# Seeding a PSUM accumulation with a ScalarE copy in place of a VectorE addition

## The chip, the core and the metric

The kernel runs on one core of a Trainium2 chip. TensorE (PE in the rows) multiplies matrices and writes PSUM; its weight loads are listed apart as PEld. VectorE (DVE) and ScalarE (ACT) work on SBUF and PSUM, GpSimd (POOL) on SBUF, and SyncE (SP) issues most transfers. Each engine takes its own instructions in order and waits on semaphores for the others. The metric is the device time of one execution in microseconds, the median of three runs.

## What is computed

The input `x` has the shape 4 x 3072 x 256. A two-dimensional Fourier transform over the last two axes gives 3072 tokens of 256 values in each of 4 batches. Two blocks of products follow:

```
X = fft(fft(x, axis=1), axis=2).real
xk = mu_k * X + (1 - mu_k) * X_prev        # X_prev: the token before
xr = mu_r * X + (1 - mu_r) * X_prev
k = max(xk @ w_k, 0)                       # 256 -> 1024
y = sigmoid(xr @ w_r) * (k * k @ w_v)      # 1024 -> 256
h = y @ w_in                               # 256 -> 2048
out = (h - tanh(h)) @ w_out                # 2048 -> 256
```

## The kernel before, in words

The Fourier transform comes first (to some 90 us). Phase 1 (some 95 to 640 us) computes `y`, phase 2 (to the end) computes `out`. Both phases go through 12 pairs of token blocks; a pair is two blocks of 512 tokens. A **step** is one call of `quad`: it makes a 2 x 2 set of result blocks, called 11, 12, 21 and 22, of the first product (`w_k` or `w_in`) with seven block products in the manner of Strassen and Winograd. Phase 1 has 4 steps for each pair, 48 in all; phase 2 has 8, 96 in all. Each block product is taken in split precision: `P(...)` issues three matmuls of 128 x 512 (lines 395 to 397), high times high, high times low, and low times high.

Every result block is bent (`bend`, L571: ReLU in phase 1, tanh in phase 2, by ScalarE), gated by VectorE (L635 for block 11, L664 for 22, L686 for 21, L687 for 12), and split into a high half by ScalarE (`hi`, L576) and a low half by VectorE (`lo`, L578). Then `second` multiplies it with the second weight (`w_v` or `w_out`): 6 matmuls for each block, into the banks `o`. `second` runs one step behind: what a step issues is its own first products, and, between these, the second products of the step before (`p`).

The order on each engine is the order in which the code is written; nothing reorders it. `self.fill()` puts the preparation of later work (splits of the left operands, weight conversion, mixing) at fixed points of the step.

The names that matter for this change:

- `X` is a PSUM bank (two of them take turns, `x0` and `x1`). It first takes the product `a11`, later `s2`, `s3` and `a22` are accumulated onto it.
- `Z` is a PSUM bank, and there is one of it only (`bank("z", "z")`). A step uses it twice: for block 11 and, from L660 on, for block 22. The last reader of block 22 is its low half, L578 `m<-z,m`; until that has run, the next step may not write `Z`.
- `s1` is an SBUF tile. L593 copies the product `a11` from `X` to it (ScalarE), before `s2` is added onto `X`.
- Block 11 is `a11` + `a12`: the product `a12` goes into `Z`, and L610 (VectorE) adds `s1` to it.

On TensorE a step begins with `a11` into `X` (3 matmuls), then the 6 matmuls of `second(p, "11")`, then `a12` into `Z` (3), then `s2` onto `X` (3). On ScalarE the copy L593 stands behind the bend of the last step's block 21 (L571 `c<-x`), and that, in phase 1, behind the high half of block 22 and what `fill` put there.

Of the kernel before, what the change touches and what calls it, by code (L numbers as in the profile page):

```python
# [392 lines left out]
def mm3(T, ps, w, m, start=True, stop=True):  # L393

    T.matmul(ps, w[0], m[0], start=start, stop=False, skip_group_check=True)  # L395
    T.matmul(ps, w[0], m[1], start=False, stop=False, skip_group_check=True)  # L396
    T.matmul(ps, w[1], m[0], start=False, stop=stop, skip_group_check=True)  # L397
# [9 lines left out]
class Kernel:  # L407
# [148 lines left out]
    def quad(self, ph, n, q, nq, S, W, w2, done, extra=None):  # L556
# [3 lines left out]
        V, A, T = self.V, self.A, self.T  # L560
        ALU, ACT = mybir.AluOpType, mybir.ActivationFunctionType
        M = {}
        def P(ps, k, start, stop=True):
            i = RIGHT[k]
            mm3(T, ps, [W[:, 0, i], W[:, 1, i]], [S[k][:, 0], S[k][:, 1]], start, stop)
        bank = lambda tag, name: self.ps.tile([128, TOK], F32, tag=tag, name=name, bufs=1)
        ctile = lambda: self.act.tile([128, TOK], F32, tag="c", name="c", bufs=4)
        stile = lambda: self.act.tile([128, TOK], F32, tag="s", name="s", bufs=3)
# [11 lines left out]
        def late(*names):  # L580
            for k in names:
                if p:
                    p["late"][k]()
        self.odd ^= 1
        X, Z = bank(f"x{self.odd}", "x"), bank("z", "z")
# [3 lines left out]
            late("t21", "g21")  # L589
        else:  # L590
            late("t21", "c12", "g21")
        s1 = stile()
        A.copy(s1, X)  # L593
        if p is None:
            self.fill()
        if ph == 1:
# [1 line left out]
        else:  # L598
            late("t12", "h21", "g12")
        self.second(p, "11")  # L600
        P(Z, "a12", True)
        Wb = None
        late("l21")
        if ph == 2:
# [2 lines left out]
        if p is None:  # L607
            Wb = bank("w", "w")
            P(Wb, "s1", True)
        V.tensor_add(Z, Z, s1)  # L610
        if ph == 2:
            late("l12")
        s2 = stile()
# [41 lines left out]
        if p is None:  # L655
            P(X, "a22", False)
            P(Wb, "s4", False)
            Z = Y
# [420 lines left out]
```

## Time and profile before

| | |
|---|---|
| median of three runs | 1638.91 us (1638.88 to 1639.13) |
| span of the profiled execution | 1637.3 us |
| TensorE busy | 1624.5 us, 99% |
| VectorE busy | 1269.1 us, 78% |
| ScalarE busy | 1137.7 us, 69% |
| GpSimd busy | 583.8 us, 36% |
| phase 1, 120 to 636 us: TensorE, VectorE, ScalarE | 516.0, 437.3, 387.3 us |
| phase 2, 670 to 1618 us: TensorE, VectorE, ScalarE | 948.0, 689.6, 626.6 us |

The profiled execution spans 1637.3 us, 1.6 us less than the median, which also holds what lies around the span. Matmuls overlap: one lasts 0.39 us and the next starts 0.227 us after it, so the distance of the starts tells what one costs. An entry such as `[0.17 <-DVE m L578]` means that the engine stood still for 0.17 us before this instruction, until that one of VectorE had ended.

### The profile page before, as it was taken

The page shows a single profiled execution, that of the slowest core. Times are in us where ns is not written, and L with a number is a line of the kernel's source. Part 1 is how long each engine was busy: PE and PEld are TensorE (multiplying, and loading weights), DVE is VectorE, ACT ScalarE, POOL GpSimd, SP SyncE. Part 2 cuts the span into 40 slices and gives each one's busy share as a digit, 9 for nine tenths or more (in the row PEclk, how much of TensorE's full clock was granted, in tenths as well). Part 3 has the DMA queues.
Part 4 walks back from the last instruction along what each step waited for, and adds up shares of the span by engine and source line. Part 5 has one row for each costly group of instructions (what it writes and reads, how often), then busy time and mean ns, then how long its engine had stood idle before and what let it go on. Part 6 is the DMA issues. An engine that isn't in the chain of part 4 may idle for free.

```text
span 1637.3 us, 21326 instructions
## 1 busy us (share of the span) xinstructions
PE 1624.5 (99%) x7478; PEld 1349.2 (82%) x7478; DVE 1269.1 (78%) x1957; ACT 1137.7 (69%) x2171; POOL 583.8 (36%) x493
## 2 busy tenths in 40 slices
PE   8999999999999999999999999999999999999998
PEld 7978888888888887888888888888888888888887
DVE  7987888888898887777777777777777777777776
ACT  5887777777777777776666666666666666666665
POOL 1156676666676776462121212121202020202000
PEclk9999999999999999999999999999999999999999
DMA  9620111111111112301010101010101010101000
GB/s 334 173 65 27 46 46 52 33 46 58 46 66 53 58 56 67 103 14 52 1 52 1 52 1 52 1 52 1 52 1 52 1 52 1 52 0 52 1 26 26
DMA packets 39612, 78.76 MB, mean 48 GB/s; under 512 B 4672, under 2 KB 11328, under 8 KB 39504
## 3 DMA queue, kind: packets, MB, share of 16 engines
q1 hardware_dynamic: 37920, 72.94, 13.3%
q0 software_dynamic: 1440, 4.46, 1.6%
q8 instruction: 58, 0.95, 0.2%
q14 instruction: 50, 0.41, 0.1%
q10 hardware_dynamic: 144, 0.00, 0.0%
HBM read 45.86 MB, written 31.52 MB: 47 GB/s over the span
## 4 chain that ended last, share of the span: by engine, by line
PE 94%; DMA 2%; DVE 1%; ACT 1%; POOL 1%; issue 1%; SPq 0%; DVEq 0%; ACTq 0%; POOLq 0%
PE o L396 16%; PE o L397 16%; PE o L395 16%; PE x L395 8%; PE x L397 8%; PE x L396 8%; PE w L397 4%; PE w L395 4%; PE w L396 4%; PE z L395 2%; PE z L397 2%; PE z L396 2%; PE r L396 1%; PE r L397 1%; PE r L395 1%; PE s L217 1%
## 5 line engine op out<-in xcount | busy, mean ns | idle before, releaser
L578 DVE TENSOR_TENSOR m<-z,m 128x512 fp32r<-128x512 f32 x288 | 198.4, 689 | 141.1 <-ACT m L576 141.1
L696 POOL TENSOR_TENSOR a<-xk,a 128x512 fp32r<-128x512 f32 x70 | 93.0, 1332 | 591.1 <-ACT a L694 591.1
L396 PE MATMUL o<-m,WO 128*128 128x512 f32 x768 | 298.9, 389 | 0.0
L397 PE MATMUL o<-m,WO 128*128 128x512 f32 x768 | 298.8, 389 | 0.0
L395 PE MATMUL o<-m,WO 128*128 128x512 f32 x768 | 298.8, 389 | 0.0
L571 ACT ACTIVATE c<-z 128x512 f32<-128x512 f32 x288 | 173.0, 601 | 141.2 <-DVE z L660 140.8
L576 ACT CAST m<-z 128x512 fp32r<-128x512 f32 x288 | 169.3, 588 | 142.9 <-DVE z L664 80.2
L696 POOL TENSOR_TENSOR s<-xk,s 128x512 fp32r<-128x512 f32 x94 | 125.4, 1334 | 186.0 <-ACT s L694 182.7
L396 PEld LDWEIGHTS o<-m,WO 128*128 128x128 f32 x768 | 144.1, 188 | 30.3 <-DVE m L578 0.3
L395 PEld LDWEIGHTS o<-m,WO 128*128 128x128 f32 x768 | 144.1, 188 | 30.0
L397 PEld LDWEIGHTS o<-m,WO 128*128 128x128 f32 x768 | 144.1, 188 | 29.8
L396 PE MATMUL o<-m,wv 128*128 128x512 f32 x384 | 149.6, 389 | 0.1
L397 PE MATMUL o<-m,wv 128*128 128x512 f32 x384 | 149.5, 389 | 0.0
L395 PE MATMUL o<-m,wv 128*128 128x512 f32 x384 | 149.5, 389 | 0.0
L664 DVE TENSOR_TENSOR z<-z,c 128x512 f32<-128x512 f32 x144 | 100.3, 697 | 61.4 <-ACT c L571 60.3
L660 DVE TENSOR_TENSOR z<-w,s 128x512 f32<-128x512 f32 x143 | 99.9, 699 | 32.7 <-PE w L397 20.0
L593 ACT COPY s<-x 128x512 f32<-128x512 f32 x144 | 84.8, 589 | 56.4 <-PE x L397 56.2
L614 ACT COPY s<-x 128x512 f32<-128x512 f32 x144 | 84.6, 587 | 53.4 <-PE x L397 52.9
L635 DVE TENSOR_TENSOR z<-z,c 128x512 f32<-128x512 f32 x144 | 100.1, 695 | 24.1 <-ACT c L571 23.3
L686 DVE TENSOR_TENSOR x<-x,c 128x512 f32<-128x512 f32 x144 | 99.5, 691 | 10.6 <-ACT c L571 10.4
L687 DVE TENSOR_TENSOR c<-c 128x512 f32<-128x512 f32 x96 | 66.9, 696 | 49.8 <-ACT c L571 49.8
L578 DVE TENSOR_TENSOR m<-x,m 128x512 fp32r<-128x512 f32 x144 | 98.7, 686 | 2.7
(214 smaller groups left out, 4040.6 us busy)
## 6 DMA issues: line engine op xcount, KB each, us to landing
spill<-r SPq DMA_DIRECT2D x48, 256.0 KB, 2.5
xk<-spill SPq DMA_DIRECT2D x48, 256.0 KB, 5.4
out<-o SPq DMA_DIRECT2D x22, 512.0 KB, 2.6
raw<-w_in SPq DMA_DIRECT2D x32, 128.0 KB, 2.3
cv<-w_out SPq DMA_DIRECT2D x16, 256.0 KB, 3.5
wf<-wf SPq DMA_DIRECT2D x16, 256.0 KB, 2.7
xr<-x SPq DMA_DIRECT2D x3, 1024.0 KB
xr<-x SPq DMA_DIRECT2D x5, 512.0 KB
```

The costliest lines, as they stand in the source:

```text
L395: T.matmul(ps, w[0], m[0], start=start, stop=False, skip_group_check=True)
L396: T.matmul(ps, w[0], m[1], start=False, stop=False, skip_group_check=True)
L397: T.matmul(ps, w[1], m[0], start=False, stop=stop, skip_group_check=True)
L571: A.activation(t, src, ACT.Tanh if ph == 2 else ACT.Relu)
L576: A.copy(M[blk][:, 0], g)
L578: V.tensor_sub(M[blk][:, 1], g, M[blk][:, 0].bitcast(F32))
L593: A.copy(s1, X)
L635: gate(Z, Z, t11)
L660: V.tensor_add(Z, Wb, s3)
L664: gate(Z, Z, t22)
L686: g21=lambda: gate(X, X, st["t21"]), h21=lambda: hi("21", X), l21=lambda: lo("21", X),
L696: eng.tensor_sub(S[name][:, 1], src(), S[name][:, 0].bitcast(F32))
```

## The change

From the second step on, ScalarE copies the product `a11` from `X` straight into the bank `Z` (no tile `s1`), the three matmuls of `a12` are issued without the start flag, so that they accumulate on the copy, and the addition L610 is gone. The first step (`p is None`) stays as it was.

```
-        s1 = stile()
-        A.copy(s1, X)
+        if p is None:
+            s1 = stile()
+            A.copy(s1, X)
+        else:
+            A.copy(Z, X)
...
         self.second(p, "11")
-        P(Z, "a12", True)
+        P(Z, "a12", p is None)
...
-        V.tensor_add(Z, Z, s1)
+        if p is None:
+            V.tensor_add(Z, Z, s1)
```

Lines behind the change stand 3 or 4 further down: the copy is L596 in the changed kernel, L614 becomes L618, L635 becomes L639.

On TensorE, at the place where a step of phase 1 (the eleventh) multiplies `a12` into `z`. Before:

```order
L397 MATMUL o_2169<-m_2216,wv 128x512
L395 MATMUL z<-a_1804,TK 128x512 [waits DVE_49]
L396 MATMUL z<-a_1804,TK 128x512
L397 MATMUL z<-a_1804,TK 128x512
L395 MATMUL x<-s_1999,TK 128x512 [waits Activation_49]
```

The same place in the changed kernel:

```order
L397 MATMUL o_2152<-m_2198,wv 128x512
L395 MATMUL z<-a_1794,TK 128x512 [waits Activation_49]
L396 MATMUL z<-a_1794,TK 128x512
L397 MATMUL z<-a_1794,TK 128x512
L395 MATMUL x<-s_1985,TK 128x512
```

The order of the matmuls is the same; the wait for ScalarE has moved from the product `s2` three matmuls up to `a12`, and takes the place of a wait for VectorE.

On ScalarE, at the copy of the same step. Before:

```order
L576 CAST m_2260<-z 128x512 [waits DVE_49]
L694 CAST a_2264<-xk 128x512
L571 ACTIVATE c<-x 128x512 [waits PE_49,Activation_49]
L593 COPY s<-x 128x512 [waits PE_49,Activation_49]
L576 CAST m_2285<-x 128x512 [waits DVE_49]
L614 COPY s<-x 128x512 [waits PE_49,Activation_49]
```

The same place in the changed kernel:

```order
L576 CAST m_2242<-z 128x512 [waits DVE_49]
L698 CAST a_2246<-xk 128x512
L571 ACTIVATE c<-x 128x512 [waits PE_49,Activation_49]
L596 COPY z<-x 128x512 [waits DVE_49,PE_49]
L576 CAST m_2266<-x 128x512 [waits DVE_49]
L618 COPY s<-x 128x512 [waits PE_49]
```

The copy stands where it stood; it now also waits for VectorE, that is for the last reader of `z`.

## Rows read from the trace of the kernel before

**Rows 1.** The page: busy time, share and instructions of each engine.

```profile
PE 1624.5 (99%) x7478; PEld 1349.2 (82%) x7478; DVE 1269.1 (78%) x1957; ACT 1137.7 (69%) x2171; POOL 583.8 (36%) x493
```

**Rows 2.** Stretches of phases 1 and 2: length, busy time of each engine, PE clock.

```profile
120.00:636.00 516.00, 516.00 (x2272) 424.93 (x2271) 437.27 (x654) 387.34 (x720) 349.48 (x283) 1.00 0.15 50
670.00:1618.00 948.00, 948.00 (x4184) 784.97 (x4183) 689.58 (x1046) 626.60 (x1136) 182.26 (x151) 1.00 0.08 27
```

**Rows 3.** Waits of the weight loads: total us, times, longest.

```profile
PEld z L395 <- DVE m L578: 3.6, 15, 0.6
PEld x L395 <- ACT s L593: 2.0, 5, 0.7
```

**Rows 4.** Groups of ScalarE by line, phase 1, then phase 2: busy, mean ns | idle before.

```profile
L593 ACT COPY s<-x 128x512 f32<-128x512 f32 x47 | 27.8, 591 | 0.0
...
L593 ACT COPY s<-x 128x512 f32<-128x512 f32 x95 | 55.9, 588 | 56.2 <-PE x L397 56.2
```

**Rows 5.** Timeline of a step of phase 2: start, duration, engine, line, operation.

```profile
902.73 0.69 DVE L578 TENSOR_TENSOR m<-z,m 128x512 fp32r<-128x512 f32 x1
903.72 0.39 PE L397 MATMUL x<-a,TI 128*128 128x512 f32 x1
904.14 0.59 ACT L593 COPY s<-x 128x512 f32<-128x512 f32 x1 [0.45 <-PE x L397]
905.08 0.19 PEld L395 LDWEIGHTS z<-a,TI 128*128 128x128 f32 x1
```

**Rows 6.** Timeline of the eleventh step of phase 1.

```profile
207.10 0.59 ACT L593 COPY s<-x 128x512 f32<-128x512 f32 x1
207.19 0.68 DVE L578 TENSOR_TENSOR m<-z,m 128x512 fp32r<-128x512 f32 x1
207.93 0.19 PEld L395 LDWEIGHTS z<-a,TK 128*128 128x128 f32 x1 [0.17 <-DVE m L578]
208.27 0.39 PE L396 MATMUL z<-a,TK 128*128 128x512 f32 x1
208.51 0.59 ACT L576 CAST m<-x 128x512 fp32r<-128x512 f32 x1 [0.82 <-DVE x L686]
```

**Rows 7.** Timeline of phase 1, the tenth step, and one near the end.

```profile
196.29 0.59 ACT L593 COPY s<-x 128x512 f32<-128x512 f32 x1
196.44 0.39 PE L395 MATMUL z<-a,TK 128*128 128x512 f32 x1
...
590.36 0.59 ACT L593 COPY s<-x 128x512 f32<-128x512 f32 x1
590.51 0.39 PE L395 MATMUL z<-a,TK 128*128 128x512 f32 x1
```

**Rows 8.** Timeline of two more steps of phase 1.

```profile
172.24 0.69 DVE L578 TENSOR_TENSOR m<-z,m 128x512 fp32r<-128x512 f32 x1 [0.58 <-ACT m L576]
172.58 0.60 ACT L593 COPY s<-x 128x512 f32<-128x512 f32 x1
173.32 0.39 PE L395 MATMUL z<-a,TK 128*128 128x512 f32 x1
...
230.58 0.59 ACT L593 COPY s<-x 128x512 f32<-128x512 f32 x1
231.24 0.39 PE L395 MATMUL z<-a,TK 128*128 128x512 f32 x1
```

**Rows 9.** Timeline of the first step of phase 2.

```profile
649.17 0.19 PEld L395 LDWEIGHTS z<-a,TI 128*128 128x128 f32 x1 [0.44 <-DVE m L578]
649.71 0.58 ACT L593 COPY s<-x 128x512 f32<-128x512 f32 x1
650.35 0.19 PEld L395 LDWEIGHTS x<-s,TI 128*128 128x128 f32 x1 [0.65 <-ACT s L593]
650.68 0.39 PE L396 MATMUL x<-s,TI 128*128 128x512 f32 x1
```

**Rows 10.** Groups of VectorE by line, phase 1, then L681 in phase 2.

```profile
L610 DVE TENSOR_TENSOR z<-z,s 128x512 f32<-128x512 f32 x48 | 33.1, 689 | 0.0
L681 DVE TENSOR_TENSOR w<-w,s 128x512 f32<-128x512 f32 x47 | 32.3, 688 | 0.0
L687 DVE TENSOR_TENSOR w<-w,c 128x512 f32<-128x512 f32 x46 | 32.0, 696 | 19.4 <-ACT c L571 19.4
L660 DVE TENSOR_TENSOR z<-w,s 128x512 f32<-128x512 f32 x46 | 32.0, 696 | 18.7 <-PE w L397 18.7
...
L681 DVE TENSOR_TENSOR c<-w,s 128x512 f32<-128x512 f32 x96 | 66.2, 690 | 3.5
```

## Prediction

> **What bounds the kernel now.** I read the page first, then the busy time by stretch, then the waits of TensorE, then the timeline around the copy in both phases. TensorE is busy for 99% of the span [rows 1], and inside both phases without a break: 516.0 of 516.0 us and 948.0 of 948.0 us, at a granted clock of 1.00 (the 2.4 GHz level) [rows 2]. VectorE, at 78%, has room. So VectorE work that goes away gives nothing back by itself; only a wait of TensorE that goes or comes changes the time. Of such waits there are few around this place: the weight load of `a12` waits for the low half of block 22 in 15 steps, 3.6 us in all, and that of `s2` waits for the copy L593 in 5 steps, 2.0 us [rows 3]. Weight loads run ahead of the matmuls, so the matmuls lost less than that.
>
> The second thing to see is that the copy is a different thing in the two phases. In phase 2 ScalarE stands idle for 56.2 us in front of its 95 copies, waiting for the product: the copy starts as soon as it can. In phase 1 it is never idle in front of the 47 copies: they come late, out of a full queue [rows 4].
>
> **What goes.** 143 additions L610 of 0.689 us [rows 10] leave VectorE, 98.5 us in all. No TensorE wait names L610. Behind it in phase 1 VectorE waits 19.4 us in front of L687 for ScalarE, and 18.7 us in front of L660 for TensorE [rows 10]; the freed time turns into more of that idleness. I cost the removal at nothing; the cover is TensorE's unbroken row, and it needs no other. The bend of block 11, which read `Z` behind L610, stands in ScalarE's queue behind the next copies and starts when these are done.
>
> **What comes: a wait of TensorE for the copy.** Before, the copy had to be over by the product `s2`, three matmuls (0.68 us) behind `a12`. Now it has to be over by `a12` itself, and it may not begin until the low half of block 22 has read `Z`. Queued behind the waiting matmul is all of TensorE's work; behind the waiting copy, on ScalarE, the high half of block 21.
>
> The price of the hand-over comes from two places. In the eleventh step the low half ends at 207.19 + 0.68 = 207.87, and the second matmul of `a12` starts at 208.27 [rows 6]; one spacing of 0.227 earlier puts the first at 208.04, 0.17 after the release. In the first step of phase 2 the copy ends at 649.71 + 0.58 = 650.29 and the second matmul of `s2` starts at 650.68 [rows 9]: 650.45, again 0.16. I take 0.17.
>
> The copy itself now writes PSUM; no row of before shows ScalarE do that. The nearest rows are VectorE's addition L681, 688 ns into PSUM in phase 1 and 690 ns into SBUF in phase 2 [rows 10]: the destination makes no difference. I take the copy's own 0.59 us, with 0.50 and 0.63 as bounds (the addition's 0.69 is VectorE's own pace, so only part of that distance).
>
> The Trainium skill (Perfetto Trace Analysis, section Optimizing Scalar/DVE Operations) gives ScalarE an access overhead of about 93 ns on SBUF and 51 ns on PSUM, and says that the profiled latency holds about twice that; as an estimate from that page, the copy would take 0.51 to 0.55 us and the sum below would come out 2 to 4 us smaller. No row here shows ScalarE write PSUM, and the VectorE pair shows no such difference.
>
> *Phase 2, 95 steps behind its first.* The low half ends at 903.42, before the product is there; the copy starts at 904.14 and ends at 904.73; the weight load of `a12` comes at 905.08 [rows 5]. 0.35 us are left over, the hand-over to the weight load costs 0.06 (650.29 to 650.35 [rows 9]), so 0.29 is spare. The steps repeat every 10.20 us with the same numbers. Cost nothing, unless the copy grew beyond 0.88 us. Only the step after the first, at 659.6, has its copy late, by 0.29.
>
> *The first step of phase 2* already waits for the copy, at `s2` [rows 9]. The wait moves three matmuls up, so it costs these three: 0.68.
>
> *Phase 1, 47 steps.* I went through all 47 in the timeline; they are of four sorts.
> - 12 steps where the low half ends after the copy has begun and `a12` already waited for it, or nearly so [rows 6]. The copy moves behind the low half: 207.87 + 0.03 + 0.59 + 0.17 = 208.66, against 208.04 before: 0.62 late. On ScalarE the copy ends at 208.49, and the next instruction did not start before 208.51 anyway.
> - 15 steps where the copy begins just before `a12`: 196.29 + 0.59 + 0.17 = 197.05 against 196.44, 0.61 late; likewise 590.36 + 0.76 = 591.12 against 590.51 [rows 7].
> - 11 steps with part of that: 172.93 + 0.03 + 0.59 + 0.17 = 173.72 against 173.32, 0.40 late [rows 8].
> - 9 steps with next to nothing: 230.58 + 0.76 = 231.34 against 231.24, 0.1 late [rows 8]; four of the nine not late at all.
>
> Where `s2` already waited for the copy only the shift of 0.68 counts. With that the first two sorts, 27 steps, give 16.8 us (0.62 each), the 11 give 4.2 (0.38 each), the 9 give 0.5: 21.5 us for phase 1.
>
> Does a step's lateness stay lost, or does ScalarE catch up while TensorE stands? The copy of the next step hangs on a chain that starts behind the place of the stall: L660 waits for TensorE's `w` (18.7 us of idle time in 46 steps [rows 10]), then come bend, gate, high half, the filled-in cast, the bend of block 21, and the copy. When TensorE is 0.6 us late this chain starts 0.6 us late too. So each step pays anew, and I take the sum as it is.
>
> **The sum.** 21.5 + 0.7 + 0.3 = 22.5 us. The stalls that were counted among [rows 3] and now lie under the copy's wait are mostly taken off above; I round down to 22. Against the profiled execution: 1637.3 + 22 = 1659.3 us of span; with the 1.6 us around it, 1661 us beside the median of 1638.9: 1.3% slower. A copy of 0.50 us takes 0.09 off some 43 late steps, 3.9 us; one of 0.63 adds 1.7. A chain that runs faster by 0.15 us a step, because VectorE's queue in front of L660 is shorter, takes off up to 7; more collisions with filled-in work may add 3. That makes 11 to 27 us, 1650 to 1666.
>
> **The rivals.**
> - *VectorE's relief pulls the chain forward, not slower.* In about half the steps of phase 1 L660 shows no idle time, so VectorE's queue may be what it starts from. If the removed 0.69 us came off there, low half, bend and copy would all come up to 0.69 us earlier, just as much as they are now late. It decides from 0.6 us a step on; then all but the ends vanish: 0 to 3 us, 1639 to 1642. Against it: the 19.4 us that VectorE waits in front of L687 [rows 10] lie between the removed addition and L660, so the time is lost before it gets there. 5%.
> - *Only half of it: partial relief together with a short copy.* If the chain came 0.25 us earlier in all steps and the copy took 0.50, the 27 steps keep 0.28 each (7.6) and the rest nearly nothing: 8 to 9 us with the ends, 1647. 8%.
> - *The copy into PSUM is so slow that phase 2 waits too.* It takes a copy beyond 0.88 us. At 1.0 us phase 1 pays 0.41 more in 43 steps (18 us) and phase 2 pays 0.12 in 95 (11 us): 22 + 29 = 51 us, 1690. The VectorE pair speaks against it. 4%.
> - *The change doesn't do what it says:* ruled out by the built order, in which 143 copies go into `z`, 142 of them with a wait for VectorE, and only one addition is left.
>
> **How the numbers follow.** The forecast, a new wait in most steps of phase 1, has 81%, and its time is 1661. Half of it has 8%, relief 5%, the slow copy 4%; 2% is for what I don't see. The range 1650 to 1667 holds the forecast with both bounds of the copy's price and leaves the rivals out, who have under 20% together. Within 0.2% (3.3 us, about what a measurement of this kernel can tell from no change) lies the relief rival: 5%; faster 2%; slower 93%.
>
> **What would show it right or wrong.** In the profile of the changed kernel, the weight load of `z` waits for ScalarE's L596 in some 43 steps of phase 1, about 20 us in all; the wait of `s2` for the copy is gone; TensorE is no longer busy throughout 120 to 636 us, and phase 1 is some 21 us longer, while each step of phase 2 still takes 10.20 us. The copy shows 0.55 to 0.60 us. VectorE loses some 98 us of busy time and shows more idle time in front of L691 (the former L687). I am wrong if phase 1 keeps its length, if the wait for the copy is short because the chain in front of it starts earlier, or if the copy takes another time than it took into SBUF.

## The result

The changed kernel takes 1659.49 us (median, 1659.29 to 1659.58) against 1638.99 us of before on the same chip: 1.0125 times as long, with a 95% interval of 1.0111 to 1.0140. That is 20.5 us more; the forecast was 22 more, 1661, with a range of 1650 to 1667.

The profiled execution spans 1657.8 us, 20.5 more than before. The page and the busy time by stretch (length, then busy time of PE, PEld, DVE, ACT, POOL, then the granted clock) answer to [rows 1, 2]:

```profile
PE 1633.3 (99%) x7478; PEld 1347.7 (81%) x7478; DVE 1200.6 (72%) x1814; ACT 1137.9 (69%) x2171; POOL 582.2 (35%) x493
```

```profile
120.00:636.00 516.00, 507.19 (x2190) 407.62 (x2189) 405.09 (x590) 375.24 (x695) 335.95 (x269) 1.00 0.15 48
...
690.00:1638.00 948.00, 948.00 (x4184) 784.98 (x4183) 642.78 (x952) 626.52 (x1136) 181.88 (x151) 1.00 0.08 27
```

VectorE has 143 instructions fewer and 68.5 us less busy time (1269.1 - 1200.6; the prediction said some 98, which counts each addition in full, while in a row of instructions each overlaps its neighbours). In phase 2 TensorE does the same 4184 matmuls in 948 us as before. In phase 1 it gets through 2190 in the stretch in which it did 2272: 82 matmuls of 0.227 us, 18.6 us of work, no longer fit in. The page still says 99% for TensorE; the loss is to be seen in the number of matmuls and in the waits, and the granted clock is 1.00 in both phases. Waits of TensorE and of its weight loads (total, times, longest), to be read beside [rows 3]:

```profile
PE z L395 <- ACT z L596: 11.1, 26, 1.2
...
PEld z L395 <- ACT z L596: 29.6, 43, 1.6
...
PEld x L395 <- ACT s L618: 0.4, 1, 0.4
PEld x L395 <- ACT s L594: 0.4, 1, 0.4
```

The 15 waits of `a12` for the low half are gone, and so are those of `s2` for the copy, but for the first step's (L594); the row of L618 is a wait for another copy, that of `s2`. 43 waits of `a12` for the copy have come, 42 of them in phase 1, as the prediction named them, but these add up to 28.0 us, where it had some 20; it took the loss of the matmuls for the waits of their weight loads. The weight load stands up to 0.22 us ahead of its matmul, so up to 43 times 0.22 of the 29.6 us (9.5) are no loss; the 20.1 that are left are about the loss.

The copy by phase (groups of ScalarE: busy, mean ns | idle before), for [rows 4]:

```profile
L596 ACT COPY z<-x 128x512 f32<-128x512 f32 x47 | 27.7, 590 | 9.7 <-DVE m L578 9.7
...
L596 ACT COPY z<-x 128x512 f32<-128x512 f32 x95 | 54.1, 570 | 58.8 <-PE x L397 58.5 <-DVE m L578 0.2
```

In phase 1 it now waits 9.7 us in all for the low half of block 22; in phase 2 still only for the product, but for 0.2 us. Three places in the timeline show the sorts of the prediction. The eleventh step, whose copy has moved behind the low half ([rows 6] before):

```profile
210.79 0.68 DVE L578 TENSOR_TENSOR m<-z,m 128x512 fp32r<-128x512 f32 x1
...
211.56 0.57 ACT L596 COPY z<-x 128x512 f32<-128x512 f32 x1 [0.75 <-DVE m L578]
...
212.18 0.19 PEld L395 LDWEIGHTS z<-a,TK 128*128 128x128 f32 x1 [0.83 <-ACT z L596]
...
212.53 0.40 PE L396 MATMUL z<-a,TK 128*128 128x512 f32 x1
```

The low half ends at 211.47, the copy runs from 211.56 to 212.13, and the second matmul of `a12` starts at 212.53; one spacing earlier is 212.30, 0.17 behind the copy, the hand-over of the prediction. The tenth step, whose copy has no wait of its own and is simply late ([rows 7]), and a step of phase 2 ([rows 5]):

```profile
199.27 0.60 ACT L596 COPY z<-x 128x512 f32<-128x512 f32 x1
...
199.92 0.19 PEld L395 LDWEIGHTS z<-a,TK 128*128 128x128 f32 x1 [0.76 <-ACT z L596]
...
924.58 0.57 ACT L596 COPY z<-x 128x512 f32<-128x512 f32 x1 [0.49 <-PE x L397]
...
925.52 0.19 PEld L395 LDWEIGHTS z<-a,TI 128*128 128x128 f32 x1
```

In phase 2 the copy ends at 925.15 and the weight load comes at 925.52: 0.37 us left over, no wait, and the steps still follow each other every 10.20 us.

### The profile page after: what moved, and what is told of

Its sections match the earlier page's. It is cut to its first block, busy times and chain, and to the rows that moved or that the text cites. A ratio compares the mean times of both kernels' runs of the same rounds, so it can differ in the third digit from the quotient of the medians.

```text
span 1657.8 us, 21275 instructions
## 1 busy us (share of the span) xinstructions
PE 1633.3 (99%) x7478; PEld 1347.7 (81%) x7478; DVE 1200.6 (72%) x1814; ACT 1137.9 (69%) x2171; POOL 582.2 (35%) x493
## 4 chain that ended last, share of the span: by engine, by line
PE 83%; DVE 7%; ACT 6%; issue 2%; DMA 2%; POOL 0%; SPq 0%; DVEq 0%; ACTq 0%; POOLq 0%
PE o L396 13%; PE o L395 13%; PE o L397 13%; PE x L397 7%; PE x L395 7%; PE x L396 7%; PE w L397 3%; PE w L396 3%; PE w L395 3%; PE z L395 3%; PE z L396 2%; PE z L397 2%; ACT c L571 1%; ACT z L596 1%; ACT m L576 1%
## 5 line engine op out<-in xcount | busy, mean ns | idle before, releaser
L639 DVE TENSOR_TENSOR z<-z,c 128x512 f32<-128x512 f32 x144 | 100.3, 696 | 57.6 <-ACT c L571 57.6
L618 ACT COPY s<-x 128x512 f32<-128x512 f32 x144 | 84.8, 589 | 68.9 <-PE x L397 68.9
L596 ACT COPY z<-x 128x512 f32<-128x512 f32 x143 | 82.5, 577 | 68.4 <-PE x L397 58.5
L690 DVE TENSOR_TENSOR x<-x,c 128x512 f32<-128x512 f32 x144 | 99.4, 691 | 10.6 <-ACT c L571 10.5
L691 DVE TENSOR_TENSOR c<-c 128x512 f32<-128x512 f32 x96 | 66.6, 694 | 50.2 <-ACT c L571 49.9
```

What stands on the lines that cost most here:

```text
L596: A.copy(Z, X)
L639: gate(Z, Z, t11)
L690: g21=lambda: gate(X, X, st["t21"]), h21=lambda: hi("21", X), l21=lambda: lo("21", X),
```

## The experiments

Each is one edit of the changed kernel or of the kernel before. Ratios are against the kernel before on the same chip.

**Which phase loses the time.** The accumulation on the copy in phase 2 only:

```
+        seed = p is not None and ph == 2
+        if seed:
+            A.copy(Z, X)
+        else:
+            s1 = stile(); A.copy(s1, X)
...
+        P(Z, "a12", not seed)
...
+        if not seed:
+            V.tensor_add(Z, Z, s1)
```

> Only the 96 steps of phase 2 accumulate on the copy; phase 1 stays as it was before. Theory (the time is lost where ScalarE's copy comes late, in phase 1 alone): 1639.2 us, that is before plus 0.2 for the first step of phase 2, and every later step still 10.20 us. Rival (some of the 20.5 us comes from the accumulation on the copy itself, or from phase 2): 1645 us or more, since 95 of 143 changed steps are here.

Measured: 1638.58 us, ratio 0.9997 (0.9988 to 1.0007). The 96 steps of phase 2 cost nothing, and the VectorE work that they save (45.7 us of busy time by the page, 1269.1 to 1223.4) brings nothing.

The same with `ph == 1`:

> Only the 47 steps of phase 1 accumulate on the copy; phase 2 stays as it was before. Theory: the whole loss, 1659.3 us. Rival (the loss is spread over all changed steps): a third of it, some 1646 us.

Measured: 1659.35 us, ratio 1.0125 (1.0110 to 1.0140): all of the loss with a third of the changed steps.

**The removal alone.** In the kernel before the addition is left out from the second step on, and nothing else is changed.

> The kernel before without VectorE's addition from the second step on (block 11 is then the product a12 alone; its other half is left out). Theory (the removed VectorE work hides behind TensorE): 1639.0 us, no change. Rival (the freed VectorE time pulls the chain to the low half of block 22 forward): 1637 us or less, since 15 weight loads wait 3.6 us for that low half before.

Measured: 1638.35 us, ratio 0.9999 (0.9989 to 1.0008). The 15 waits for the low half are still there:

```profile
PEld z L395 <- DVE m L578: 3.4, 15, 0.5
```

So the removed additions give nothing back, and the low half comes no earlier. The rival of VectorE's relief falls for the kernel as it was.

**The wait without the change.** The kernel before, addition and SBUF tile kept; on TensorE the product that waits for the copy goes where the change put the wait:

```
-        P(Z, "a12", True)
+        if p is None or ph == 2:
+            P(Z, "a12", True)
...
         P(X, "s2", False)
+        if p and ph == 1:
+            P(Z, "a12", True)
```

> The kernel before with VectorE's addition and the SBUF tile kept; only the order on TensorE differs in phase 1: the product s2, which has to wait for the copy, goes ahead of a12. So the wait for the copy stands where the change put it, but the copy does not have to wait for the low half of block 22. Theory: of the four sorts of steps, the 15 whose copy begins just before a12 pay 0.61 us again, 6 pay 0.4, 5 about 0.1, the 12 where the copy had to go behind the low half pay nothing; less some 2 us that the changed kernel did not lose either at its uneven steps: before plus 11 us, 1650. Rival (the wait's place costs nothing, the seeding does): 1639.

Measured: 1651.47 us, ratio 1.0078 (1.0062 to 1.0093), 12.9 us more than before, 2 more than expected. The waits for the copy are there without any seeding:

```profile
PEld x L395 <- ACT s L593: 20.0, 29, 1.3
```

I took the lateness of each step from the distance of the first `a12` matmuls of two neighbouring steps, against the kernel before, and summed it by the step's place among the four of its pair (us, all of phase 1; the last four rows belong to edits further down):

```
                          1st     2nd     3rd     4th    steps of a pair
changed kernel            2.9     7.1     7.0     3.3
the wait only             2.8    10.7    -0.5     0.3
low half first            3.5     7.1     0.2     3.2
copy first                2.1     5.3     6.9     3.0
both                      2.5     5.2     0.0     2.6
more cover                0.2     5.5     0.3     6.8
```

The third and fourth steps, where the copy has to go behind the low half in the changed kernel, lose next to nothing here, as expected: their loss comes from the one bank `Z`, not from the place of the wait. The second steps lose more than in the changed kernel, 1.2 us instead of 0.6 in three of them. In one of these VectorE's kept addition, now waiting for the later `a12`, is followed by a filled-in conversion of 1.79 us, and the gate of block 12 (L690) comes behind both:

```profile
233.62 0.70 DVE L613 TENSOR_TENSOR z<-z,s 128x512 f32<-128x512 f32 x1 [0.28 <-PE z L397]
234.23 1.79 DVE L456 SCALAR_TENSOR_TENSOR cva<-raw,cva 128x512 int32<-128x512 int32 x1
235.94 0.69 DVE L690 TENSOR_TENSOR w<-w,c 128x512 f32<-128x512 f32 x1
```

That is where the missing 2 us most likely went; I did not test it apart.

**What makes the copy late.** Three edits of the changed kernel in phase 1. First the low half of block 22 ahead of the filled-in work:

```
         if ph == 1:
-            self.fill()
             lo("22", Z)
+            self.fill()
```

> The changed kernel, and in phase 1 the low half of block 22 goes ahead of the filled-in work instead of behind it. Theory (in 12 steps the copy had to wait for a low half that stood behind a filled-in VectorE operation of 0.7 to 1.8 us): these steps lose their 0.65 us, the others keep theirs: 1659.5 - 7.2 = 1652.3 us. Rival (the copy is late from ScalarE's queue alone): 1659.5, no change.

Measured: 1653.40 us, ratio 1.0087 (1.0073 to 1.0100), 6.1 us less than the changed kernel. The third steps are free of loss (0.2 us of 7.0), one of them:

```profile
209.48 0.69 DVE L578 TENSOR_TENSOR m<-z,m 128x512 fp32r<-128x512 f32 x1 [0.65 <-ACT m L576]
...
210.09 1.43 DVE L828 SCALAR_TENSOR_TENSOR xk<-xt,mut,y 128x512 f32<-128x512 f32 x1
210.35 0.60 ACT L596 COPY z<-x 128x512 f32<-128x512 f32 x1
211.04 0.19 PEld L395 LDWEIGHTS z<-a,TK 128*128 128x128 f32 x1
```

The low half is over at 210.17, before ScalarE gets to the copy, and the weight load has no wait. The first steps lose 0.6 us more than in the changed kernel (3.5 for 2.9). The expected 7.2 took 12 steps for the sort that gains; ten third steps gained.

Second, the copy ahead of the bend and the gate of block 21 on ScalarE:

```
         P(X, "a11", True)
-        if ph == 1:
-            late("t21", "g21")
-        else:
+        if ph == 2:
             late("t21", "c12", "g21")
         if p is None: ...
         else:
             A.copy(Z, X)
+        if ph == 1:
+            late("t21", "g21")
```

> The changed kernel, and in phase 1 the copy into z goes ahead of the bend and the gate of the last step's block 21, which stood in front of it on ScalarE (0.49 us). Theory (the low half of block 22 ends only 0.18 us before the copy could begin in some 22 steps, and behind that point in 17): the copy gains 0.15 us in these 22 steps and 0.4 in two: 1659.5 - 4 = 1655.5 us. Rival (ScalarE's queue alone makes it late): 0.49 us in 26 steps, 1647 us.

Measured: 1656.50 us, ratio 1.0105 (1.0091 to 1.0119), 3.0 us less. The bend took 0.49 us of ScalarE's queue, but most second steps got only 0.10 to 0.14 us back (in the tenth step 0.64 became 0.50), and the third steps did not move: the low half, which ends 0.18 us before the copy began, is the next thing to wait for. The rival, ScalarE's queue alone, would have given 12 us, four times as much.

Third, both:

> Both moves: low half of block 22 ahead of the filled-in work, and the copy ahead of the bend of block 21, in phase 1. Theory (two causes that add): 1659.5 - 7.2 - 4 = 1648.3 us. Rival (one cause behind both, ScalarE's queue or the low half): no better than the better one of the two alone.

Measured: 1649.56 us, ratio 1.0063 (1.0050 to 1.0077), 9.9 us less: 6.1 and 3.0 add. The trace shows the larger part of the 10.5 us that are left: in 44 of the 47 steps of phase 1 ScalarE now stands idle in front of the copy until the low half is over, and VectorE stands idle in front of the low half, until the high half is. The tenth step:

```profile
196.30 0.69 DVE L578 TENSOR_TENSOR m<-z,m 128x512 fp32r<-128x512 f32 x1 [0.65 <-ACT m L576]
...
197.08 0.57 ACT L594 COPY z<-x 128x512 f32<-128x512 f32 x1 [0.29 <-DVE m L578]
...
197.70 0.19 PEld L395 LDWEIGHTS z<-a,TK 128*128 128x128 f32 x1 [0.64 <-ACT z L594]
```

This step still loses 0.50 us, and the copy could begin 0.29 us earlier if it did not share a bank with block 22. Taken step by step, this idle time, up to what the step loses, adds up to 7.6 us; so much at most is an estimate of what the one bank `Z` costs here. A second bank for `Z` was not tried.

**The low half first, without the change.** The first of the three edits, in the kernel before:

> The kernel before, with the low half of block 22 ahead of the filled-in work in phase 1. Theory: the waits of the weight load of a12 for that low half (3.6 us in 15 steps) go, but they cost the matmuls only some 0.03 us each: 1638.5 us, a gain of 0.5. Rival (these waits are TensorE time in full): 1635.5.

Measured: 1642.27 us, ratio 1.0022 (1.0013 to 1.0031): slower by 3.3 us, where both theories had a gain. The waits of `a12` for the low half fell from 3.6 to 2.4 us, those of `s2` for the copy rose from 2.0 to 3.4, and new ones came at `w`:

```profile
PEld w L395 <- DVE m L578: 4.7, 9, 0.8
PEld x L395 <- ACT s L593: 3.4, 11, 0.6
...
PEld z L395 <- DVE m L578: 2.4, 8, 0.6
```

The filled-in work, moved behind the low half, now delays what follows it on VectorE; in front of one of those waits, for the low half of block 12, that queue has no idle time:

```profile
256.59 1.74 DVE L824 SCALAR_TENSOR_TENSOR xk<-xt,mut,y 128x512 f32<-128x512 f32 x1
258.25 0.69 DVE L687 TENSOR_TENSOR w<-w,c 128x512 f32<-128x512 f32 x1
258.85 0.68 DVE L635 TENSOR_TENSOR z<-z,c 128x512 f32<-128x512 f32 x1
259.59 0.69 DVE L578 TENSOR_TENSOR m<-w,m 128x512 fp32r<-128x512 f32 x1
```

With the same edit on the changed kernel, where the addition is gone, no such wait at `w` shows. That may be the freed 0.69 us of VectorE; but TensorE also comes late in most second steps there, which gives VectorE time as well, and the two were not taken apart.

**More cover for the copy,** that is more TensorE work in front of the product that waits for it. The changed kernel, with three of the six matmuls of block 22 ahead of `a12`, and `s3` behind the products of `r`, in phase 1 (the third argument of `second` names the halves of the second weight to multiply with):

```
         self.second(p, "11")
+        if ph == 1:
+            self.second(p, "22", (0,))
         P(Z, "a12", p is None)
...
-        self.second(p, "22")
+        self.second(p, "22", (1,) if ph == 1 else (0, 1))
...
-        if s3 is None:
+        if s3 is None and ph == 2:
             P(X, "s3", False)
...
             r = extra(bank(f"x{1 - self.odd}", "r"))
+        if s3 is None and ph == 1:
+            P(X, "s3", False)
```

> The changed kernel, with more TensorE work in front of a12 in phase 1: the first three of the six matmuls of the last step's block 22 go ahead of a12 (0.68 us), and, so that s3 keeps its distance from s2, the product s3 goes behind the products of r. The copy, the low half and their queues stay as they are. Theory (a12 comes at most 0.66 us too early, and that is the whole loss): the waits of a12 for the copy all but vanish in phase 1, 1640 us, with some 1 us left at the first steps of both phases. Rival (a slower chain of VectorE and ScalarE sets phase 1 once the copy stands in it): the waits come back elsewhere, at s3 or at w, and the kernel stays above 1650 us.

Measured: 1651.19 us, ratio 1.0071 (1.0057 to 1.0084). The waits of `a12` fell from 29.6 to 7.4 us, 1.6 of them in one step, and others came, 7.5 us at `w` and, where there had been 0.8, 4.0 at `o`:

```profile
PEld w L395 <- DVE m L578: 7.5, 11, 0.7
PEld z L395 <- ACT z L596: 7.4, 17, 1.6
PEld o L396 <- DVE m L578: 4.0, 11, 0.5
```

Both theories got half. The cover does hide the copy in most steps; but phase 1 then waits for the low halves of other blocks. In the third steps the low half of block 12 ends 5.86 us behind `a12`, as in the changed kernel (5.87), and `w`, which the cover has brought three matmuls closer to `a12`, now has to wait for it. Waits came at `w`, as the rival said, and at `o`, not at `s3`, and the time is near the rival's.

> The same cover, and both earlier moves too (low half of block 22 ahead of the filled-in work, copy ahead of the bend of block 21). Theory: nothing more to gain, since the cover already hides the copy: 1640 us. Rival (lateness beyond the cover is left): lower than with the cover alone by up to 2 us.

Measured: 1658.38 us, ratio 1.0114 (1.0099 to 1.0130), 7 us slower than the cover alone. Neither theory had this. New waits stand at `r`, which the cover moved up and which goes into the other bank of `X`; that bank is free only when the low half of block 21 has read it, and the copy ahead of the bend puts block 21 back. In the tenth step the gate of block 21 has to wait 1.21 us for the bend, where with the cover alone it waits 0.33:

```profile
PEld r L395 <- DVE m L578: 14.1, 26, 0.7
...
200.94 0.70 DVE L694 TENSOR_TENSOR x<-x,c 128x512 f32<-128x512 f32 x1 [1.21 <-ACT c L571]
```

No version tried is measurably faster than the kernel before. The one with the accumulation in phase 2 only ties with it, with 96 additions less on VectorE.

## Why the prediction was right, point by point

**Removal at nothing:** right, shown by leaving the addition out (0.9999). VectorE's idle time in front of the gate of block 12 in phase 1 rose from 19.4 [rows 10] to 52.0 us. The removal alone, in the run that leaves the addition out, brings it to 32.1; the other 20 us are about what TensorE's new waits added to the phase:

```profile
L691 DVE TENSOR_TENSOR w<-w,c 128x512 f32<-128x512 f32 x46 | 32.2, 699 | 52.0 <-ACT c L571 51.9
```

**Phase 2 at nothing:** right, 0.9997 with phase 2 alone.

**Its first steps at 1.0 us:** too high. From the last step of phase 1 on, the lateness goes 1.16, -0.83, -0.16: 0.2 in all. In the kernel before TensorE also waited here for the copy of `s2`, 1.1 us in 3 waits over the whole run; in the changed one there is one of 0.4. Two of these three stood at this place (0.43 and 0.29 us), and the new wait lies over them, which the sum did not take off. The row of before:

```profile
PEld x L395 <- ACT s L614: 1.1, 3, 0.4
```

**Phase 1 at 21.5 us:** 20.3 measured, by the sorts of the prediction (us):

```
steps                                         predicted   measured
12, copy behind the low half, and
15, copy just before a12                       16.8        15.9 (8.3 and 7.6)
11, part of it                                  4.2         4.2
 9, next to nothing                             0.5         0.2
```

The sum of the first two sorts is closer than its parts: at 0.62 each the 12 cost 0.9 more and the 15 cost 1.7 less. Of the 12, nine lost 0.66 to 0.68. One, the second step of phase 1, is not of that sort: its copy began 0.29 us behind the first matmul of `a12` before the change, and it lost 1.12, where the shift alone would be 0.68. Of the 15, two lost 0.06 us instead of some 0.67, and one near the start 0.38 instead of 0.67 with 0.4 given back in the step behind it. In one of the two the chain did start earlier than before. VectorE's rows there, before and after:

```profile
453.86 1.29 DVE L452 TENSOR_SCALAR cv<-cv 128x512 f32<-128x512 f32 x1
455.07 0.69 DVE L687 TENSOR_TENSOR w<-w,c 128x512 f32<-128x512 f32 x1
```

```profile
468.30 0.70 DVE L691 TENSOR_TENSOR w<-w,c 128x512 f32<-128x512 f32 x1 [1.26 <-ACT c L571]
```

Before, the gate of block 12 came right behind a conversion that overran; after, VectorE was free 1.26 us ahead of it. Counted from the first `a12` matmul of its step (451.31, and 465.09 after), the gate came 0.55 us earlier (3.76 and 3.21). That the removed addition did it is not shown. The wait only, which keeps the addition, loses as little in the same two steps (0.05 and 0.06 us); and with the addition left out and nothing else changed, this gate comes earlier too (3.25), but the copy stays 0.07 us ahead of `a12`, where it was. So the relief rival has at most two steps in 47, worth 1.2 us.

**Each step pays anew:** right. The lateness does not fade over the phase, as it would if ScalarE caught up: of the second steps of the pairs seven pay 0.61 to 0.66, the tenth step of phase 1 0.64 and the forty-second still 0.61; of the third steps, nine in ten from the third pair on pay 0.60 to 0.68. The chain is tied to TensorE earlier than the prediction had it: in 24 of 47 steps of the kernel before L660 had no idle time, but in front of L691 VectorE now stands idle in 44 of 48 steps, until ScalarE, which has waited for TensorE's `s2`, has bent block 12.

**The copy's price:** 0.59 us taken; 0.590 us in phase 1 and 0.570 in phase 2, where nothing runs in front of it. The 0.51 to 0.55 us worked out from the Trainium skill (Perfetto Trace Analysis, section Optimizing Scalar/DVE Operations) was not seen: into PSUM the copy is 18 ns shorter than into SBUF in phase 2 (588 [rows 4] to 570) and 1 ns in phase 1 (591 to 590).

**Why it was late** was stated as two causes, the low half and ScalarE's queue. The edits show that the low half is the larger one: moving it up gave 6.1 us, moving the copy up 3.0, and both together 9.9. With both moved the copy still waits for the low half in 44 of 47 steps, so the bank that block 22 and the copy share is what comes next.

## What to carry to other kernels

Before moving an addition from one engine into another's accumulation, look at where the result of the copy is waited for: an operand of an addition behind the product may come late, a seed must be there before it, and the bank must be free before that; here the copy waited for the bank's last reader in 44 of 47 steps even when both queues were out of the way. On an engine that is busy throughout, count the distance between the copy's end and the first matmul that needs it, step by step; 0.37 us to spare costs nothing in 95 steps, 0.6 us too little costs 0.6 in each. Work taken off an engine that waits anyway gave nothing back here (0.9999); what it is worth where other work fills the queue was not shown.

## What the runs showed of the hardware

A ScalarE copy of 128 x 512 from PSUM took 0.570 us into PSUM and 0.588 into SBUF in phase 2, where ScalarE was idle before it; in phase 1 the means are 0.590 and 0.591, most copies standing right behind another instruction. A matmul whose weight load waited for ScalarE started some 0.17 us behind the copy's end, as it does behind VectorE. TensorE's granted clock stayed at 1.00 (2.4 GHz) through a phase with a stall of 0.3 to 0.7 us in most steps.
